# One of 32 V loads of a decode attention kernel sent as sixteen transfers of eight partitions

## The chip, the cores and the metric

The kernel runs on one core of one Trainium2 chip. The metric is the device time of one execution in microseconds. Before the change the median of three runs is 197.03 us (196.81 to 197.30). A profile of one execution on the chip belongs to it; that execution took 196.93 us.

The engines are named as in the profile: PE (matrix multiply, with PEld for its weight loads), DVE (vector), ACT (activations), POOL and SP. SP computes nothing here, its instructions issue the large DMA transfers. Sixteen DMA engines move the data. A time written as a position, such as 105.84, counts from the start of the profiled span.

## What is computed

One decode step for eight sequences. Attention over the last 1024 positions of a K/V cache with 8 heads of K and V, 16 heads of Q and a head size of 256, mixed by a sigmoid gate with a small MLP:

```python
W = min(4096, max(256, Sk // 4))                 # 1024
k = jnp.repeat(k_cache[:, :, Sk - W:, :], rep, axis=1)
v = jnp.repeat(v_cache[:, :, Sk - W:, :], rep, axis=1)
scores = jnp.einsum("bhqd,bhkd->bhqk", q, k) * (Dh ** -0.5)
p = _softmax(scores, axis=-1)
o = jnp.einsum("bhqk,bhkd->bhqd", p, v)
a = o.transpose(0, 2, 1, 3).reshape(B, Sq, Hq * Dh) @ wo
...
h = _gelu(_layernorm(x) @ w1 + b1)
b = h @ w2 + b2
g = _sigmoid((x * gate_w).sum(-1, keepdims=True))
return g * a + (1 - g) * b
```

All tensors are bfloat16. The parts of K and V that are read are 64 MB; the weights are another 13.6 MB.

## The kernel before

The work on the cache is cut into 32 units for K and 32 for V. A unit is one K/V head (`g`, 0 to 7) of two sequences (`u`, 0 to 3, `TB` = 2), numbered `n = 4 g + u`. One load brings one unit: a tile `kv` of 128 partitions, each with 16 positions of 256 numbers, 8 KB. Partition `2 r + t` holds positions `16 r` to `16 r + 15` of sequence `t`, so the source is walked as 64 blocks `r` by 2 sequences `t`, each a contiguous run of 8 KB. The tiles come from a pool of twelve (`NKV`). Only the last V unit is sent in two transfers of half the width.

All of these loads are issued by SP, in the order of the list `units` (L170 to L179): K of unit `n`, after every fourth K the part of `wo` for one head (`W`, 448 KB), then V of unit `n - 5`. V of unit 16 thus stands between K of unit 21 and K of unit 22. `issue_to` issues as many as there are free tiles: twelve at the start, and one more for each unit of K or V that the PE has used up. SP works its list in order; an instruction that waits holds all later ones.

An issue on SP waits for two things. The framework gives the transfers eight completion semaphores in turn, so a transfer waits until the one eight places before it has landed. And a load that takes a tile over waits until PE has read the tile's last content.

The main loop (L528) goes over half units, one sequence each: `transposes` turns K with the PE into PSUM, and DVE copies it out (L392, L397); `scores` multiplies it with Q (L418); once per head come maximum, exponent and sum; eleven half units later `pv` multiplies V with the probabilities (L490); once per head `o_proj` adds the head's part of the output (L515). At the end one DVE operation adds the MLP's part (L555) and two transfers store the result (L559).

ACT's queue carries four small transfers at the start (`x_sb` and `gw_sb` of eight rows, `b1_sb` and `b2_sb` of one row) and one of the two output halves at the end.

Of the kernel before, what the change touches and what calls it, by code (L numbers as in the profile page):

```python
# [16 lines left out]
def kernel(  # L17
# [15 lines left out]
    nc = tc.nc  # L33
    P = nc.NUM_PARTITIONS

    B, Sq, D = A_x.shape
    _, Hkv, Sk, Dh = A_k_cache.shape
# [4 lines left out]
    kv0 = Sk - W  # L42
# [3 lines left out]
    TB = 2  # L46
    NC = W * TB // P
# [14 lines left out]
    NU = NBU * Hkv  # L62
    NSTEP = NU * TB
    SPG = NBU * TB
    LAG = 3
    NKV = 12
    NEG = -1.0e30


# [18 lines left out]
    big = ctx.enter_context(tc.tile_pool(name="big", bufs=1))  # L88
    kvpool = ctx.enter_context(tc.tile_pool(name="kvpool", bufs=NKV))
    ktpool = ctx.enter_context(tc.tile_pool(name="ktpool", bufs=3))  # L90
# [45 lines left out]
    KV = {}  # L136

    def load(kind, n):
        t = kvpool.tile([P, NC, Dh], BF16, tag="kv", name="kv")
        src = A_k_cache if kind == "K" else A_v_cache  # L140
        g, u = divmod(n, NBU)
        parts = TB if (kind, n) == ("V", NU - 1) else 1
        w = NC // parts
        for q in range(parts):
            nc.sync.dma_start(
                t[:, q * w : (q + 1) * w, :].rearrange("p c d -> p (c d)"),
                src[u * TB : (u + 1) * TB, g, kv0:Sk, :].rearrange(
                    "t (r c) d -> r t c d", c=NC
                )[:, :, q * w : (q + 1) * w, :].rearrange("r t c d -> r t (c d)"),
            )  # L150
        KV[kind, n] = t

    nc.scalar.dma_start(x_sb[:], xf)
    nc.scalar.dma_start(
# [27 lines left out]
    def issue_to(k):  # L182
        while pos[0] < len(units):
            kind, n = units[pos[0]]
            if kind == "W":
                r0 = n * NKH * P
                nc.sync.dma_start(
                    wo_sb[n][:].rearrange("p (i j) n -> p i (j n)", i=rep),
                    A_wo[r0 : r0 + NKH * P, :].rearrange(
                        "(i p j) n -> p i (j n)", i=rep, j=NJ  # L190
                    ),
                )
            else:
                if pos[1] == k:
                    return
                load(kind, n)
                pos[1] += 1
            pos[0] += 1

    issue_to(NKV)  # L200

# [5 lines left out]
    nc.gpsimd.affine_select(  # L207
        out=cross[:], in_=cross[:], compare_op=ALU.is_equal, fill=NEG, base=0,
        pattern=[[-1, TB], [0, rep]], channel_multiplier=1,
# [145 lines left out]
    for c in range(DC + 1):  # L355
        for k in range(NQ):
            if c < DC:
                w, xs = wq_sb[:, c, k * P : (k + 1) * P], xT[:, c, :]
            else:
                h, kk = divmod(k, NQ // 2)  # L360
                w, xs = wq_t[:, kk * P : (kk + 1) * P], xT[:, DC + h, :]
# [147 lines left out]
    def o_proj(g):  # L509
        ot = OT[g]  # L510
        for i in range(rep):
            for h in range(NJ):
                k = i * NJ + h
                for j in range(CT):
                    nc.tensor.matmul(  # L515
                        A_ps[CP * j : CP * j + NB, :],
                        lhsT=ot[:].rearrange("p j (b i) -> p j i b", i=rep)[:, h, i, :],
                        rhs=wo_sb[g][:, k, j * DN : (j + 1) * DN],
                        start=(g == 0 and k == 0),
                        stop=(g == Hkv - 1 and k == NKH - 1),  # L520
                        tile_position=(0, CP * j),
                        skip_group_check=True,
                    )
# [4 lines left out]
    for n in range(LAST):  # L528
# [5 lines left out]
        g, r = divmod(n, SPG)  # L534
# [8 lines left out]
        if m >= 0:  # L543
# [6 lines left out]
            if m % SPG == 0 and m > 0:  # L550
                o_proj(m // SPG - 1)
        issue_to(NKV + done)
    o_proj(Hkv - 1)
# [36 lines left out]
```

## Time and profile before

| What | Value |
|---|---|
| median of three runs | 197.03 us |
| the profiled execution, its own time | 196.93 us |
| its span, first to last instruction | 195.1 us |
| PE busy | 166.0 us (85%) |
| DVE busy | 109.6 us (56%) |
| read from HBM | 77.68 MB, 398 GB/s over the span |
| packets of all DMA queues | 12770 |
| a K load, from issue to landing (median of 32) | 19.7 us |
| a V load (median of 31) | 18.2 us |
| the V load of unit 16 | issued at 105.84 us |

The page of the profile begins with busy times by engine, then shows the span in 40 equal slices with a digit per slice (9 stands for 90% or more), then the DMA queues with packets, bytes and share of the engines' time, then the chain of work that ended last, followed backwards from the last instruction. Views of the trace add the order of the instructions on one engine (timeline), who waited for whom (waits), and sums over chosen stretches (windows). A row of a timeline gives start, duration, engine, line, operation and tiles; SPq is SP's sequencer as it issues a transfer, and the duration is that of the issue, not of the data.

### The profile page before, as it was taken

Reading aid. Unit: us, or ns where it says so; the run is one execution under the profiler, and the core shown is the slowest. Engines: PE = TensorE matmul, PEld = TensorE weight load, DVE = VectorE, ACT = ScalarE, POOL = GpSimd, SP = SyncE. Lnnn points to the kernel's source line nnn. Section 1 sums busy time; section 2 is a strip of 40 time slices with the busy share of each in tenths; the row PEclk is TensorE's granted clock in tenths of the full one; section 3 lists DMA queues with packets and bytes.
Section 4 is the critical chain, followed back from the end, with each engine's and each line's share of the span. In section 5 each row is a group of like instructions: output and inputs, shape, how many; then the busy total and the mean of one; then the engine's idle time right before and its main releaser. Section 6 shows DMA issues by size and latency. Waiting matters only on the chain.

```text
span 195.1 us, 7576 instructions
## 1 busy us (share of the span) xinstructions
PE 166.0 (85%) x3528; PEld 155.2 (80%) x3528; DVE 109.6 (56%) x246; ACT 6.4 (3%) x13; POOL 2.7 (1%) x15
## 2 busy tenths in 40 slices
PE   0777899988799999799998997999689969898663
PEld 0665899988798899689997997889588969797561
DVE  3422189995476357745596468547384637665301
ACT  4100000000000000000000000000000000000000
POOL 5000000000000000000000000000000000000000
PEclk9999999997855559755597599559797888879555
DMA  5999999999999999999999999999999999999940
GB/s 207 410 436 422 418 417 431 422 425 417 422 425 422 422 425 423 422 420 425 427 423 418 425 423 423 422 417 426 425 422 427 420 423 423 428 423 420 404 189 8
DMA packets 12770, 78.16 MB, mean 401 GB/s; under 512 B 1330, under 2 KB 3523, under 8 KB 4164
## 3 DMA queue, kind: packets, MB, share of 16 engines
q1 hardware_dynamic: 12688, 77.67, 95.5%
q8 instruction: 27, 0.44, 0.8%
q10 hardware_dynamic: 52, 0.02, 0.1%
q14 instruction: 3, 0.02, 0.0%
HBM read 77.68 MB, written 0.01 MB: 398 GB/s over the span
## 4 chain that ended last, share of the span: by engine, by line
DMA 74%; PE 22%; SPq 1%; DVE 1%; issue 1%; ACT 0%; ACTq 0%
DMA kv<-in_A_k_cache_dram 58%; PE ktp L392 13%; DMA wo_sb<-in_A_wo_dram 9%; DMA wq_sb<-in_A_wq_dram 7%; PE grp L418 3%; PE grp L490 3%; PE A_ps L515 1%; DVE kt L397 0%; SPq L167 0%; PE grp L407 0%; DVE rz L477 0%; DVE res L555 0%; SPq L164 0%; PE grp L460 0%; SPq L159 0%
## 5 line engine op out<-in xcount | busy, mean ns | idle before, releaser
L397 DVE COPY kt<-ktp 128x1024 bf16<-128x1024 bf16 x128 | 84.8, 688 | 48.9 <-PE ktp L392 48.4
L392 PE MATMUL ktp<-ident,kv 128*128 128x128 bf16 x1024 | 89.4, 258 | 8.7 <-DMA kv<-in_A_k_cache_dram 8.7
L392 PEld LDWEIGHTS <-kv 128*128 128x128 bf16 x1024 | 77.7, 118 | 12.3 <-DMA kv<-in_A_k_cache_dram 9.4
L490 PE MATMUL grp<-e,kv 128*128 128x4 bf16 x1024 | 35.1, 165 | 5.9 <-DVE rz L477 4.6
L490 PEld LDWEIGHTS <-kv 128*128 128x128 bf16 x1024 | 32.1, 100 | 7.4 <-issue 5.0
L418 PE MATMUL grp<-qT,kt 128*128 128x4 bf16 x1024 | 36.9, 166 | 0.9 <-issue 0.5
L418 PEld LDWEIGHTS <-kt 128*128 128x128 bf16 x1024 | 34.8, 101 | 2.3 <-issue 1.0
L467 ACT ACTIVATE e<-grp 128x256 bf16<-128x256 f32 x8 | 3.1, 384 | 165.1 <-PE grp L460 165.1
L515 PE MATMUL A_ps<-wo_sb,ot 128*8 128x224 bf16 x64 | 7.0, 366 | 0.3 <-DMA wo_sb<-in_A_wo_dram 0.3
L477 DVE RECIPROCAL rz<-grp 128x16 f32<-128x16 f32 x8 | 2.0, 254 | 7.9 <-PE grp L472 5.9
L472 PEld LDWEIGHTS <-onesb 128*128 128x128 bf16 x128 | 4.7, 102 | 1.9 <-issue 1.2
L299 PE MATMUL h_ps<-yT,w_sb 128*128 128x8 bf16 x42 | 4.2, 194 | 0.8 <-DMA w_sb<-in_B_w_dram 0.8
L331 PE MATMUL b_ps<-w_sb,hT 128*8 128x224 bf16 x28 | 2.8, 388 | 2.4 <-DVE b_ps L327 2.4
L472 PE MATMUL grp<-e,onesb 128*128 128x16 bf16 x128 | 4.7, 174 | 0.0
L501 DVE TENSOR_TENSOR ot<-grp,rz 128x32 bf16<-128x32 f32 x8 | 1.5, 192 | 5.2 <-PE grp L490 5.2
L299 PEld LDWEIGHTS <-w_sb 128*128 128x128 bf16 x42 | 3.6, 152 | 0.9 <-DMA w_sb<-in_B_w_dram 0.9
L263 PE MATMUL tp<-ident,y_sb 8*128 8x8 bf16 x3 | 0.2, 170 | 4.7 <-DVE y_sb L244 4.7
L331 PEld LDWEIGHTS <-hT 128*8 128x8 bf16 x28 | 1.8, 121 | 3.0 <-DVE hT L322 2.2
L460 PE MATMUL grp<-diag,onesb 128*128 128x256 bf16 x8 | 2.6, 321 | 1.9 <-DVE diag L454 1.8
L431 DVE TENSOR_REDUCE pm<-grp 128x16 f32<-128x256 f32 x8 | 3.3, 416 | 1.3 <-PE grp L418 1.3
L263 PEld LDWEIGHTS <-y_sb 8*128 8x128 bf16 x3 | 0.2, 103 | 4.7 <-DVE y_sb L244 4.7
L515 PEld LDWEIGHTS <-ot 128*8 128x8 bf16 x64 | 2.8, 103 | 1.2 <-DVE ot L501 0.4
(77 smaller groups left out, 52.4 us busy)
## 6 DMA issues: line engine op xcount, KB each, us to landing
kv<-in_A_k_cache_dram SPq DMA_DIRECT2D x32, 1024.0 KB, 19.7
kv<-in_A_v_cache_dram SPq DMA_DIRECT2D x31, 1024.0 KB, 18.2
wo_sb<-in_A_wo_dram SPq DMA_DIRECT2D x8, 448.0 KB, 18.3
wq_sb<-in_A_wq_dram SPq DMA_DIRECT2D x3, 1024.0 KB, 11.4
w_sb<-in_B_w_dram SPq DMA_DIRECT2D x1, 1568.0 KB, 9.2
w_sb<-in_B_w_dram SPq DMA_DIRECT2D x1, 1344.0 KB, 5.9
kv<-in_A_v_cache_dram SPq DMA_DIRECT2D x2, 512.0 KB, 19.8
wq_t<-in_A_wq_dram SPq DMA_DIRECT2D x1, 512.0 KB
```

The lines of the kernel that those rows point to most:

```text
L299: nc.tensor.matmul(o, lhsT=cols(w1_sb[:, c, h * FH : (h + 1) * FH]), rhs=yT[:, c, :], start=(c == 0), stop=False,)
L331: nc.tensor.matmul(b_ps[CP * j : CP * j + NB, 0:DN], lhsT=M["hT"][:, k * NB : (k + 1) * NB] if k < NF else onesb[0:1, 0:NB], rhs=w2_sb[:, ...
L392: nc.tensor.transpose(ktp[:, c * P : (c + 1) * P], K[:, h * HC + c, j * P : (j + 1) * P], ident[:],)
L397: nc.vector.tensor_copy(kt[:, j, :], ktp[:])
L418: nc.tensor.matmul(G[g][:, s : s + RU], lhsT=kt[:, j, c * P : (c + 1) * P], rhs=qT[:, j, g, bu * TB : (bu + 1) * TB, :].rearrange("p t i - ...
L431: nc.vector.reduce_max(pm[:], G[g][:, S0 : S0 + NC * R].rearrange("p (c r) -> p r c", r=R), axis=AXIS.X,)
L460: nc.tensor.matmul(G[g][:, S0 : S0 + NC * R].rearrange("p (c r) -> p c r", c=NC), lhsT=onesb[:], rhs=diag[g % 2][:].unsqueeze(1).to_broadc ...
L467: nc.scalar.activation(e[:], G[g][:, S0 : S0 + NC * R], ACT.Exp)
L472: nc.tensor.matmul(G[g][:, Z0 : Z0 + R], lhsT=onesb[:], rhs=E[g][:, c * R : (c + 1) * R], start=False, stop=(c == NC - 1), skip_group_chec ...
L477: nc.vector.reciprocal(rz[:], G[g][:, Z0 : Z0 + R])
L490: nc.tensor.matmul(G[g][:, o : o + RU], lhsT=V[:, cc, :].rearrange("p (q j) -> p j q", j=NJ)[:, j, :], rhs=E[g][:, cc * R + bu * RU : cc * ...
L515: nc.tensor.matmul(A_ps[CP * j : CP * j + NB, :], lhsT=ot[:].rearrange("p j (b i) -> p j i b", i=rep)[:, h, i, :], rhs=wo_sb[g][:, k, j * ...
```

## The change

In `load`, one unit of V, number 16 of 32, is sent as sixteen transfers. Piece `i` fills partitions `8 i` to `8 i + 7` over their whole width of 8 KB, which is 64 KB, and reads four blocks `r` of the two sequences. The bytes and their places are the same. The other loads keep their shape; their source is only written in another way.

```diff
     NKV = 12
+
+    BY_ROWS = {("V", NU // 2)}
+    ROWS = 8
...
         g, u = divmod(n, NBU)
+        rows = src[u * TB : (u + 1) * TB, g, kv0:Sk, :].rearrange(
+            "t (r c) d -> r t (c d)", c=NC
+        )
+        KV[kind, n] = t
+        if (kind, n) in BY_ROWS:
+            for p0 in range(0, P, ROWS):
+                nc.sync.dma_start(
+                    t[p0 : p0 + ROWS, :, :].rearrange("p c d -> p (c d)"),
+                    rows[p0 // TB : (p0 + ROWS) // TB],
+                )
+            return
         parts = TB if (kind, n) == ("V", NU - 1) else 1
         w = NC // parts
         for q in range(parts):
             nc.sync.dma_start(
                 t[:, q * w : (q + 1) * w, :].rearrange("p c d -> p (c d)"),
-                src[u * TB : (u + 1) * TB, g, kv0:Sk, :].rearrange(
-                    "t (r c) d -> r t c d", c=NC
-                )[:, :, q * w : (q + 1) * w, :].rearrange("r t c d -> r t (c d)"),
+                rows[:, :, q * w * Dh : (q + 1) * w * Dh],
             )
-        KV[kind, n] = t
```

In the built program SP has sixteen instructions in place of one at that point. Each writes 8 partitions by 4096 numbers and reads 4 by 2 by 4096. Each takes the next of the eight semaphores, so piece `i` waits for the transfer eight places before it, pieces 8 to 15 wait for pieces 0 to 7, and K of unit 22 waits for piece 8. The first piece alone waits for the tile's last use by PE. On PE, the first weight load that reads this tile waits for eight semaphores in place of one. The other engines' instructions are unchanged.

## The prediction

> **What bounds the kernel now.** I read the page's head, slices and chain first, to learn which engine sets the end.
>
> ```profile
> span 195.1 us, 7576 instructions
> ...
> DMA  5999999999999999999999999999999999999940
> ...
> q1 hardware_dynamic: 12688, 77.67, 95.5%
> ...
> DMA 74%; PE 22%; SPq 1%; DVE 1%; issue 1%; ACT 0%; ACTq 0%
> ```
>
> The 16 DMA engines are full from the second slice to the 38th, and 77.67 MB on SP's queue q1 take 95.5% of their time. What makes one of these engines busy longer moves the end, unless that engine has slack. So I read the queue's pace and what its issues wait for (timeline of SP: start, duration; then SP's waits: total us, times, longest).
>
> ```profile
> 77.38 0.53 SPq L145 DMA_DIRECT2D kv<-in_A_k_cache_dram  x1
> 79.81 0.54 SPq L145 DMA_DIRECT2D kv<-in_A_v_cache_dram  x1
> 82.25 0.53 SPq L145 DMA_DIRECT2D kv<-in_A_k_cache_dram  x1
> 84.68 0.54 SPq L145 DMA_DIRECT2D kv<-in_A_v_cache_dram  x1
> 87.12 0.54 SPq L145 DMA_DIRECT2D kv<-in_A_k_cache_dram  x1
> ```
>
> ```profile
> SPq L145 <- DMA kv<-in_A_k_cache_dram: 58.4, 30, 3.5
> SPq L145 <- DMA kv<-in_A_v_cache_dram: 39.7, 21, 3.4
> ...
> SPq L145 <- PE ktp L392: 5.1, 14, 0.6
> ```
>
> SP waits for earlier DMAs (98.1 us), hardly for PE's release of a slot (5.1 us). In the built program every transfer on SP waits for the one eight places before it, so eight are in flight. Four loads are issued in 87.12 - 77.38 = 9.74 us: 2.435 us each. A load is 128 rows of 8 KB, eight for each of 16 engines, so **a row holds an engine 0.304 us**.
>
> The windows of the tail (stretch, its length, ACT's busy time, PE clock, DMA share, GB/s) show that the engines do not finish together:
>
> ```profile
> 184.00:185.00 1.00, 0.00 (x0) 0.50 0.94 382
> 186.00:187.00 1.00, 0.00 (x0) 0.50 0.55 225
> 188.00:189.00 1.00, 0.00 (x0) 0.50 0.54 209
> 190.00:191.00 1.00, 0.00 (x0) 0.50 0.14 47
> ```
>
> Half of them are through at about 185, the other half between 189 and 191; 0.14 of 16 is the last two. The final load counts as landed when the last of them is done.
>
> **The change, part by part.** (1) Removed: one issue of 0.53 us on SP, and one load's eight rows on each engine, 2.43 us of stream. (2) Added: sixteen issues of eight rows. What the trace has of eight rows is ACT's gw_sb, and the outputs at the end:
>
> ```profile
> 1.43 0.28 ACTq L154 DMA_DIRECT2D gw_sb<-in_gate_w_dram  x1
> ```
>
> ```profile
> q10 hardware_dynamic: 16, 0.00, 0.7%
> ```
>
> The first (ACT's timeline) prices an issue at 0.28 us; a piece has the three-step source of a K load (0.53), so 0.28 to 0.54. The second (DMA view of 192.5 to 195.1 us) is ACT's queue at the end, which carries one output half: 16 packets, eight rows of 448 B and eight completions. A transfer of eight rows thus used at most eight engines, while 128 rows use sixteen. How many does a piece use? In the built program its source is walked as 4 steps of 2 batch rows, its destination as 8 partitions. Eight if the destination decides, four if the source's four steps do; I take **four**, since a division that has to fit both sides can be no finer than four. The trace has no transfer whose two sides differ below sixteen.
>
> [...] No run here shows a transfer with unequal sides yet.
>
> (3) I take the four to be the same for every piece: ACT's two one-row transfers, b1 and b2, went through one engine, as the trace's packets (rows of one engine come 0.304 us apart) can be followed. They get 128 / 4 = 32 rows instead of eight. **Lower bound**, each row at 0.304: 32 x 0.304 = 9.73 us, less the 2.43 removed: +7.30. **Upper bound**: the eight rows of a piece go into eight neighbouring partitions, while in a 128-row load each engine has eight of the 128 to itself. If two engines that write into the same few partitions take turns, a row costs 2 x 0.304 = 0.608: 32 x 0.608 - 2.43 = +17.03. No 8 KB row of the trace has two engines there. I take **the middle**, 0.456 a row: 32 x 0.456 - 2.43 = +12.16. Reason: the engines reach the pieces displaced. The sixteen completions of the K load ahead of them (issued at 102.98) spread from 117.96 to 121.33 us, 3.4 us or eleven rows; the engine in front writes other partitions than the one behind for the first pieces, and meets it once pieces come only as older ones land.
>
> [...]
>
> (4) Slack: rows on an engine that would have finished early cost less. Following q1's packets engine by engine through the trace, the engine that carries b1 and b2 ends at 189.5, the last at 190.9: **-1.4** if that one is among the four. Bounds: 0 (the four hold the last one), -6 (all four end at 185).
>
> (5) SP and the eight in flight. Piece s0 is issued at 105.84, when the load eight before it has landed, and s7 only once K load 21 has landed (121.4); s8 to s15 wait for s0 to s7, and the next K load for s8. Behind SP's waits stand all later loads, and PE waits for these. With four engines it costs nothing extra: seven pieces of two rows are 14 x 0.304 = 4.3 us of queued work, longer than one issue and start (0.54 + about 0.5, as the output's 192.67 issue and its first packet show), and a piece takes 0.61 us, longer than its issue. The cover is the pieces' own slowness; without it (rival 2) SP's issues set the pace. The other twelve engines run dry and refill before the four are done. (6) PE: one weight load waits for eight semaphores instead of one; PE idles while K load 22 is late and then works at the stream's pace as before. The tail behind the last landing (191.2 to 195.1) stays.
>
> **Sum**: +12.16 - 1.4 = +10.8. Span 195.1 + 10.8 = 205.9. The profiled execution took 196.93, 1.83 outside its span, 0.10 under the median of 197.03. **207.7 us.**
>
> **Rivals.** *1, four engines without turns:* rows keep 0.304. +7.30 - 1.4 = +5.9, **202.8**. For it: every 8 KB row of the trace takes the same time whatever the other fifteen do. Against: these fifteen were in other partitions. *2, eight engines, rows at 0.304:* 16 x 0.304 - 2.43 = +2.43, no slack (the last two would be among eight more likely); or SP's nine issues s7 to s15 after 121.4: K load 22 starts moving at 121.4 + 9 x 0.28 (or 0.54) + 0.54 + 0.5 = 125.0 to 127.3, where it would have started at 121.3 + 2.4 = 123.7: +1.3 to +3.6. The larger of each pair: +2.4 to +3.6, **199.3 to 200.5**. For it: the output half used eight. Against: there both sides have eight steps. (Eight engines whose rows cost double come to rival 1's sum, 16 x 0.608 - 2.43 = +7.3.) *3, fewer than four engines, or all in turn:* two engines carry 64 rows, 64 x 0.304 - 2.43 - 1.4 = +15.6, **212.5**, and more with turns. Only the two batch rows of the source speak for it. *4, not slower:* pieces go to all engines in rotation (eight rows each, as before), and SP issues them fast enough that the queue does not run dry: 9c + 0.54 + 0.5 must stay under 2.4, so an issue c under 0.15 us. Then **197.0**. Against: the cheapest issue in the trace is 0.27 (b1, b2), and nothing shows a rotation. That the change does nothing is excluded: the built program has sixteen transfers there.
>
> **How the numbers follow.** Forecast 0.50 (205 to 212.5), rival 1 0.29 (202 to 204.5), rival 2 0.11, rival 3 0.06, rival 4 0.04. The range 200.5 to 212.5 holds the first two and rival 2's upper end, and leaves out some 0.18. About 0.3%, 0.6 us, can be told from no change. Faster 0.01, same 0.03, slower 0.96: only rival 4 does not end slower, and a quarter of it goes to a gain from a luckier slack of the engines.
>
> **What will show it.** Completions: a 128-row load has 16; the page's 12770 packets become 12818 with four engines for each piece (64 - 16 more), 12882 with eight, 13010 with sixteen. The windows after 122 us: a DMA share near 0.25 or less, and 107 GB/s without turns (4 x 8192 B / 0.304 us), 54 with full turns. SP's timeline: s7 at about 121.4, K load 22 at 121.4 plus half the stall. The tail: the last stretch no longer ends with two engines but with up to four. The prediction is wrong if the share stays above 0.9 between 120 and 135 us, or if K load 22 waits for PE instead of s8.

## The result and the profile after

| What | Before | After |
|---|---|---|
| median of six runs of each, in one comparison | 196.94 us (196.81 to 197.30) | 205.37 us (204.53 to 206.62) |
| ratio of the medians, 95% interval | | 1.0427 (1.0403 to 1.0452) |
| span of the profiled execution | 195.1 us | 203.4 us |
| K load 21, the last before the edit, landed at | 121.33 us | 122.44 us |
| K load 22, the next after it, issued at | 107.84 us | 128.59 us |
| K load 22, landed at | 127.62 us | 136.25 us |
| last load of `wo`, landed at | 191.21 us | 199.34 us |

The kernel became slower by 8.4 us. The page's head, slices, DMA table and chain, as they were shown of before:

```profile
span 203.4 us, 7595 instructions
...
DMA  6999999999999999999999961599999999999970
...
DMA packets 12818, 78.16 MB, mean 384 GB/s; under 512 B 1378, under 2 KB 3571, under 8 KB 4212
...
q1 hardware_dynamic: 12736, 77.67, 92.3%
...
DMA 51%; PE 35%; DVE 7%; SPq 3%; issue 2%; ACT 0%; ACTq 0%; DVEq 0%
```

The same 77.67 MB go over q1, but slices 24 to 26 (5 us each) are no longer full: 6, 1 and 5 tenths. The stream has one hole, and the rest of it runs as before. The packets are 48 more, which is 64 completions for the sixteen pieces in place of 16: four engines for each piece.

SP's timeline around the hole, and SP's last nine issues of pieces by tile (count, shortest, median and longest in ns, first and last start):

```profile
102.99 0.54 SPq L159 DMA_DIRECT2D kv<-in_A_k_cache_dram  x1
105.89 22.59 SPq L151 DMA_DIRECT2D kv<-in_A_v_cache_dram  x16
128.59 0.58 SPq L159 DMA_DIRECT2D kv<-in_A_k_cache_dram  x1
```

```profile
L151 SPq DMA_DIRECT2D kv<-in_A_v_cache_dram x9: 630/630/631, 122.5 to 127.8; - x9
```

Between K load 21 at 102.99 and K load 22 at 128.59 SP sends nothing but 1 MB of V. The first seven pieces are issued at the stream's pace, each when an earlier load has landed. The other nine are issued back to back from 122.45, 0.63 us each and 0.675 us apart, and K load 22 directly behind the last.

The windows (stretch, its length, ACT's busy time, PE clock, DMA share, GB/s) show what the engines do meanwhile:

```profile
118.00:120.00 2.00, 0.00 (x0) 1.00 0.76 295
120.00:122.00 2.00, 0.00 (x0) 0.78 0.49 152
122.00:124.00 2.00, 0.00 (x0) 0.50 0.17 61
124.00:126.00 2.00, 0.39 (x1) 0.50 0.15 61
126.00:128.00 2.00, 0.00 (x0) 0.50 0.28 78
128.00:130.00 2.00, 0.00 (x0) 0.50 0.23 86
130.00:132.00 2.00, 0.00 (x0) 0.50 0.96 274
```

From 122 to 130 us between two and five of sixteen engines work (0.15 to 0.28). They move 61 to 86 GB/s, less than the 97 GB/s at which SP issues (65,536 B in 0.675 us): the pieces pile up on their four engines. PE has no work at the end of it. Its waits (total us, times, longest), first the line of before, then those of after, and a row of PE's timeline after (in brackets the idle time ahead of it, and what ended that):

```profile
PE ktp L392 <- DMA kv<-in_A_k_cache_dram: 8.7, 8, 1.9
```

```profile
PE grp L501 <- DMA kv<-in_A_k_cache_dram: 5.9, 1, 5.9
...
PE ktp L403 <- DMA kv<-in_A_k_cache_dram: 5.2, 7, 1.4
```

```profile
134.43 0.56 PE L501 MATMUL grp<-e,kv 128*128 128x4 bf16 x16 [5.88 <-DMA kv<-in_A_k_cache_dram]
```

The view puts the long wait down to a K load, but L501 is `pv`, which reads V, and it goes on at 134.43, when K load 22 has not landed (136.25) and the last piece of V unit 16 has (134.08). So PE waits 5.9 us for the pieces; its wait for K load 22 is 0.46 us, ahead of a row at 136.29.

The end of the stream, the same kind of windows:

```profile
197.00:198.00 1.00, 0.00 (x0) 0.50 0.45 170
198.00:199.00 1.00, 0.00 (x0) 0.50 0.08 29
```

The last stretch belongs to about one engine (0.08 of 16). The sixteen completions of two loads, read from the trace's semaphore events in order of time, show the same engines' lag from the hole to the end:

```
K load 22, before:  122.86 to 124.80 (eight), 125.87 to 126.19 (seven), 127.62
K load 22, after:   134.09 to 134.49 (twelve), 135.02 135.06 135.24 136.25
last wo, before:    185.17 to 187.00 (eight), 189.59 to 191.21 (eight)
last wo, after:     196.24 to 198.01 (thirteen), 198.44 198.50 199.34
```

So two things add up at the end: thirteen engines are through 6.8 us later than the last engine before (198.01 against 191.21), and the slowest one is another 1.3 us behind them. The experiments take the two apart.

### The profile page after: what moved, and what is told of

The parts are those of the page before. It is cut to its first block, busy times and chain, and to the rows that moved or that the text cites. A ratio compares the mean times of both kernels' runs of the same rounds, so it can differ in the third digit from the quotient of the medians.

```text
span 203.4 us, 7595 instructions
## 1 busy us (share of the span) xinstructions
PE 172.2 (85%) x3528; PEld 161.2 (79%) x3528; DVE 110.3 (54%) x246; ACT 6.4 (3%) x13; POOL 2.7 (1%) x15
## 2 busy tenths in 40 slices
DMA packets 12818, 78.16 MB, mean 384 GB/s; under 512 B 1378, under 2 KB 3571, under 8 KB 4212
## 3 DMA queue, kind: packets, MB, share of 16 engines
q1 hardware_dynamic: 12736, 77.67, 92.3%
## 4 chain that ended last, share of the span: by engine, by line
DMA 51%; PE 35%; DVE 7%; SPq 3%; issue 2%; ACT 0%; ACTq 0%; DVEq 0%
DMA kv<-in_A_k_cache_dram 45%; PE ktp L403 20%; PE grp L501 6%; PE grp L429 6%; DVE kt L408 3%; DMA kv<-in_A_v_cache_dram 3%; DMA w_sb<-in_B_w_dram 3%; SPq L151 2%; PE A_ps L526 2%; DVE diag L465 1%; PE grp L471 1%; DVE rz L488 1%; DVE pm L442 0%; ACT e L478 0%; DVE mx L459 0%
## 5 line engine op out<-in xcount | busy, mean ns | idle before, releaser
L403 PE MATMUL ktp<-ident,kv 128*128 128x128 bf16 x1024 | 95.5, 268 | 7.1 <-DMA kv<-in_A_k_cache_dram 5.2
L403 PEld LDWEIGHTS <-kv 128*128 128x128 bf16 x1024 | 83.0, 123 | 10.9 <-DMA kv<-in_A_k_cache_dram 6.4
L501 PE MATMUL grp<-e,kv 128*128 128x4 bf16 x1024 | 35.4, 166 | 9.9 <-DMA kv<-in_A_k_cache_dram 5.9
L501 PEld LDWEIGHTS <-kv 128*128 128x128 bf16 x1024 | 32.6, 101 | 11.2 <-issue 10.8
L429 PEld LDWEIGHTS <-kt 128*128 128x128 bf16 x1024 | 35.5, 102 | 1.8 <-issue 0.7
```

Source lines behind the costliest of these rows:

```text
L403: nc.tensor.transpose(ktp[:, c * P : (c + 1) * P], K[:, h * HC + c, j * P : (j + 1) * P], ident[:],)
L429: nc.tensor.matmul(G[g][:, s : s + RU], lhsT=kt[:, j, c * P : (c + 1) * P], rhs=qT[:, j, g, bu * TB : (bu + 1) * TB, :].rearrange("p t i - ...
L501: nc.tensor.matmul(G[g][:, o : o + RU], lhsT=V[:, cc, :].rearrange("p (q j) -> p j q", j=NJ)[:, j, :], rhs=E[g][:, cc * R + bu * RU : cc * ...
```

## Experiments

Three mechanisms were in question when the expectations were written. One is the rows: engines that write at the same time into the same few neighbouring partitions take turns, and a row costs up to 0.608 us in place of 0.304. The second is SP: eight transfers in flight hold 512 KB in place of 8 MB when they are pieces, the queue runs dry, and K load 22 must wait for SP to issue nine pieces one by one. The third is the share: four engines have 32 rows to move while twelve have none. The expectations give these theories letters. Each edit is against the changed kernel, in the branch for V unit 16 where nothing else is said; each time stands beside the runs of the kernel before in the same comparison (196.80 to 196.89 us).

**e1_ports: the same pieces, written four partitions apart.**

```diff
+                i = p0 // ROWS
+                d0 = (i // 4) * 32 + i % 4
                 nc.sync.dma_start(
-                    t[p0 : p0 + ROWS, :, :].rearrange("p c d -> p (c d)"),
+                    t[d0 : d0 + 29 : 4, :, :].rearrange("p c d -> p (c d)"),
```

> The sixteen pieces read the same bytes in the same order on the same queue, but each fills eight partitions that lie four apart (partitions b, b+4, ... b+28 of a block of 32) in place of eight neighbours, so that the rows of one piece no longer share a group of four partitions. The V rows of unit 16 so stand in other partitions, and that part of the output is not the reference's. Theory A (rows of two engines take turns on the same few partitions, part of the forecast): the mean time of a row in the stretch 122 to 132 us falls from about 0.4-0.5 us to 0.31, and the time falls by 2 to 3 us from 205.4 to 202.5-203.5. Theory B (what costs is the nine issues on SP after K load 21 has landed, while twelve engines run dry): SP's rows stay 0.63 us, K load 22 is still issued at about 128.6, and the time stays within 1 us of 205.4. Theory C (32 rows on four engines, each at 0.304, nothing else): 199-201.

Measured 204.92 us, +8.1 (ratio 1.0403, 1.0385 to 1.0422), against +8.4 for the change. K load 22 is issued at 128.66. One window from the middle of the hole:

```profile
126.00:128.00 2.00, 0.00 (x0) 0.50 0.20 74
```

The hole is the same, and the rate in it too (78 GB/s there in the change): SP's nine issues held K load 22 as before, as the second theory expected. The rows themselves did change. Of the 8 KB rows that begin between 123.5 and 130 us, 50 of 61 take under 0.33 us here, against 36 of 58 in the change. Most of the others begin on three engines at once and take 0.69 to 0.90 us, more than the 0.608 of two engines that take turns; what holds them is not known. The last piece lands 1.0 us earlier than in the change (133.05), the last `wo` 0.6 earlier (198.77). So fewer turns in the hole gain little here, and not the 2 to 3 us that the first theory expected.

**e2_wide: sixteen transfers over all 128 partitions, 512 B of each row.** Every transfer spans all 128 partitions, as the loads before do, which land with sixteen completions; only SP's part of the change is left.

```diff
-            for p0 in range(0, P, ROWS):
+            wd = NC * Dh // 16
+            for q in range(16):
                 nc.sync.dma_start(
-                    t[p0 : p0 + ROWS, :, :].rearrange("p c d -> p (c d)"),
-                    rows[p0 // TB : (p0 + ROWS) // TB],
+                    t[:].rearrange("p c d -> p (c d)")[:, q * wd : (q + 1) * wd],
+                    rows[:, :, q * wd : (q + 1) * wd],
                 )
```

> Sixteen transfers again, but each over all 128 partitions and a sixteenth of the width (512 B rows), so every engine gets the same bytes as in the kernel before. Theory B (SP's nine issues after K load 21): nine issues of 0.54-0.68 us = 4.9-6.1 us plus 2-3 us until the first bytes; twelve and more engines dry in that time; 201-203 us. Theory C (rows on four engines) and theory A (turns): nothing left of either but short rows, 16 x 8 rows of about 0.025 us = 3.2 us in place of 2.43: 197.5-198.

Measured 203.73 us, +6.9 (1.0349, 1.0329 to 1.0369). SP's issues by tile and windows:

```profile
L152 SPq DMA_DIRECT2D kv<-in_A_v_cache_dram x9: 535/604/1178, 121.5 to 127.2; - x9
```

```profile
122.00:124.00 2.00, 0.38 (x1) 0.97 0.15 43
126.00:128.00 2.00, 0.00 (x0) 0.50 0.41 92
```

The same nine issues come after K load 21 has landed (121.50), and K load 22 is issued at 127.91. The hole is there although each transfer spans all partitions: **SP's pace alone costs 6.9 us**, somewhat more than expected and about the delay that the thirteen engines show in the changed kernel (6.8). Short rows can add little: a row of 512 B takes 0.027 us (median), 128 of them 3.5 us an engine, 1 us more than a load has before, and in the windows from 122 to 130 us the engines are busy for 0.15 to 0.64 of the time. That 6.9 and 6.8 are so close should not be pressed: in this trace, too, one engine ends late: the last `wo` lands on fifteen engines by 197.55 and on one at 198.55, although all large transfers of this kernel span the 128 partitions.

**e7_wide8: the same with eight transfers of 1 KB.**

```diff
-            wd = NC * Dh // 16
-            for q in range(16):
+            wd = NC * Dh // 8
+            for q in range(8):
```

(Against e2_wide.)

> Eight transfers over all 128 partitions, an eighth of the width each (1 KB rows), against sixteen in e2_wide. Theory B (the issues that SP still has to make once K load 21 has landed): one such issue in place of nine, K load 22 is issued before 123.5 us in place of 127.9, and most of the 6.9 us of e2_wide goes: 197-199. If the loss of e2_wide came from short rows or from the number of transfers as such, about half of it stays: 200-201.

Measured 198.77 us, +1.9 (1.0104, 1.0087 to 1.0120). One issue instead of nine stands between the landing of K load 21 and K load 22, which is issued at 121.99. The window in which the stream thins out most:

```profile
122.00:124.00 2.00, 0.38 (x1) 1.00 0.74 176
```

Eight issues less bring K load 22 forward by 5.9 us (127.91 to 121.99) and the time by 5.0. This is the second mechanism by its size.

**e3_rows16 and e4_rows32: eight pieces of sixteen partitions, and four of thirty-two.**

```diff
-    ROWS = 8
+    ROWS = 16
```

> Eight transfers of sixteen partitions. Each should use eight engines (the packets would be 12770 + 64 - 16 = 12818), 16 rows each. Theory B: only the last piece is issued after K load 21 has landed, so K load 22 is issued some 0.7 us later; with 2-3 us to the first bytes, +0.5 to +2: 197.5-199. Theory C: +2.43 on eight engines, nothing if these are the eight that run ahead: 197-199.4. Theory A: rows of two engines share a group of partitions, up to double: eight engines take up to 9.7 us: +2 to +5, 199-202.

Measured 203.41 us, +6.6 (1.0319, 1.0275 to 1.0363).

```diff
-    ROWS = 8
+    ROWS = 32
```

> Four transfers of 32 partitions, each over sixteen engines (packets 12770 + 3 x 16 = 12818), two rows per engine and piece, eight in all as before. Theory B and theory C: no loss, 196.9-197.3, since all four are issued before K load 21 lands. Theory A: the 32 partitions of a piece are eight groups of four for sixteen engines, so rows take up to double and the load up to 4.9 us in place of 2.43: up to +2.4, 198-199.4.

Measured 201.46 us, +4.7 (1.0237, 1.0218 to 1.0256). Windows of e3_rows16, then of e4_rows32:

```profile
126.00:128.00 2.00, 0.38 (x1) 0.50 1.02 250
```

```profile
120.00:122.00 2.00, 0.00 (x0) 0.50 1.09 225
...
126.00:128.00 2.00, 0.38 (x1) 0.50 0.94 225
```

With thirty-two rows nothing is dry, and the stream still loses 4.7 us: from about 118 to 128 us all engines are busy (0.94 to 1.09 in the windows) at little more than half the rate. The rows themselves take nearly twice as long (0.58 us on average between 119 and 127 us, against 0.31 before). This fits the first mechanism, and it costs more than the one load's own rows, because neighbours slow down as well: all 226 rows of 8 KB that begin in this stretch take 0.45 us or more, where the load has 128, and K load 21's last engine lands at 123.83 and at 121.33 before. In e3_rows16 SP is free 4.1 us earlier than in the change (K load 22 issued at 124.44, against 128.59). This trace is of the fastest of its four executions (201.84 us, the others 203.21 to 203.90), and is 3.3 us faster than the traced one of the change (205.14). By the medians the gain is 1.8. Once the queue is full again, busy engines (1.02) move 250 GB/s: there slow rows have taken back a part of what SP gave. Both times lie above all that the expectations had (up to 202 and 199.4), since these priced slow rows for the one load alone.

**e5_halves and e6_evenodd: two transfers of 64 partitions, neighbours in one, every second partition in the other.** Same number of transfers, same bytes, all sixteen engines busy (a share of 0.93 to 1.08 in the windows of both from 118 to 132 us).

```diff
-    ROWS = 8
+    ROWS = 64
```

> Two transfers of 64 neighbouring partitions, each over sixteen engines, four rows per engine and piece. Theory A (a group of neighbouring partitions takes rows at one engine's pace, so sixteen engines on 64 partitions run at half): as with four transfers of 32, a DMA share near 1.0 at about 225 GB/s for some 5 to 8 us; +2.4 to +4.7: 199.2-201.5. Theory B (SP's issues): one more issue, all given out long before they are due: 196.8-197.2.

```diff
-            for p0 in range(0, P, ROWS):
+            for q in range(TB):
                 nc.sync.dma_start(
-                    t[p0 : p0 + ROWS, :, :].rearrange("p c d -> p (c d)"),
-                    rows[p0 // TB : (p0 + ROWS) // TB],
+                    t[q : P - TB + q + 1 : TB, :, :].rearrange("p c d -> p (c d)"),
+                    rows[:, q, :],
                 )
```

> Two transfers of 64 partitions as well, but the even ones (one sequence) and the odd ones (the other), so that each transfer reaches over all 128 partitions. Same engines, same bytes, same number of issues as with two halves. Theory A: each transfer can be taken at the full pace, no stretch at 225 GB/s; 196.8-198. If instead smaller transfers as such are slow, the same time as with two halves.

Measured: halves 201.39 us, +4.5 (1.0236, 1.0220 to 1.0251); every second 196.88 us, ratio 1.0004 (0.9994 to 1.0013, ten runs): nothing lost. Windows of e5_halves, then of e6_evenodd:

```profile
120.00:122.00 2.00, 0.00 (x0) 0.50 1.08 233
122.00:124.00 2.00, 0.00 (x0) 0.50 0.97 225
```

```profile
120.00:122.00 2.00, 0.00 (x0) 0.72 1.02 430
122.00:124.00 2.00, 0.00 (x0) 0.50 1.03 422
```

This pair differs in which partitions are written together, and with that in what is read: half of the blocks of both sequences, or all blocks of one. Sixteen engines into 64 neighbouring partitions: 225 to 233 GB/s. Into 64 partitions spread over all 128: 422 to 430. **Turns on neighbouring partitions** are the likely reason. The order of the reads is not ruled out by this pair; e1_ports, which has the reads of the change and other partitions, speaks for the partitions (50 of 61 rows undisturbed there, against 36 of 58). How many partitions share a turn is not shown: the groups of four that the expectations of e1_ports and e4_rows32 count by are an assumption of their author, and 64 neighbouring partitions are sixteen such groups, one for each engine, yet the rate is halved here. e6_evenodd is a way to cut a load that costs nothing.

**e8_spread: SP's pace taken out.** Two pieces go behind each of eight earlier loads, into a part of `wq_sb` that is no longer used, so that the queue never holds pieces alone. The list `PIECES` takes the sixteen transfers in `load`, in place of issuing them.

```diff
...
-        t = kvpool.tile([P, NC, Dh], BF16, tag="kv", name="kv")
+        if (kind, n) in BY_ROWS:
+            t = wq_sb[:, 0, :].rearrange("p (c d) -> p c d", c=NC)
+        else:
+            t = kvpool.tile([P, NC, Dh], BF16, tag="kv", name="kv")
...
-                load(kind, n)
-                pos[1] += 1
+                if (kind, n) not in BY_ROWS:
+                    load(kind, n)
+                    pos[1] += 1
+                if (kind, n) == ("V", NU // 2 - 4):
+                    load("V", NU // 2)
+                for _ in range(2):
+                    if PIECES:
+                        nc.sync.dma_start(*PIECES.pop(0))
...
```

> The same sixteen pieces of eight partitions, but two after each of the eight loads ahead of V unit 16's place (V unit 12 to K unit 21), into memory that is free by then (a part of wq_sb), so that SP never has several pieces in a row and large loads are in flight beside them. Theory B (SP's nine issues in a row): the dry stretch goes and the time falls by 5 us or more, to 197-200.5. Theory C (32 rows on four engines): these engines still get 24 rows more, +7.3 less the 3.3 us and more that they run ahead: 199-201, the tail shows a share of a quarter. Theory A (turns) adds up to 3 us to it.

Measured 210.91 us, +14.0 (1.0716, 1.0689 to 1.0744): much worse than the change, and than any theory expected (up to some 204). Windows:

```profile
105.00:110.00 5.00, 0.00 (x0) 0.50 0.97 316
...
120.00:125.00 5.00, 0.00 (x0) 0.50 0.80 210
```

SP's pace alone can't be the story: a theory of SP only would have this kernel near the one before. Where pieces run beside full loads the rate falls to 316 GB/s with all engines busy, and the four that carry pieces fall behind: a K load issued at 122.31 lands on twelve engines by 129.12 and on four between 134.46 and 136.95. The share of 0.80 says that other engines run short of work meanwhile; a transfer that these four hold up keeps its place in flight, which would explain it.

**e9_split8: K load 22, V load 17 and K load 23 put between the eighth piece and the ninth.** SP's list then reaches the next large loads after one issue instead of nine. `PIECES` is as in e8_spread, the place of the tile as in the change.

```diff
...
+                if (kind, n) in BY_ROWS or (kind, n) == ("K", NU // 2 + 7):
+                    for _ in range(8):
+                        nc.sync.dma_start(*PIECES.pop(0))
```

> The sixteen pieces as in the change, but K unit 22, V unit 17 and K unit 23 are issued between the eighth and the ninth of them, so that large loads are queued before SP gives out the last eight. Theory B (twelve engines run dry while SP gives out nine pieces): the stretch at a share of 0.2 goes, K load 22 is issued at about 124 in place of 128.6, and the time falls to 199-202. Theory A in the form that the spread pieces showed (pieces beside running loads slow these by taking turns on their partitions; sixteen cost 14 us): eight of them beside the stream cost about 7, so 203-206, with a share of 0.9 and more at 210-330 GB/s while they run.

Measured 206.80 us, +10.0 (1.0485, 1.0443 to 1.0528), above both expected ranges. Windows:

```profile
124.00:126.00 2.00, 0.38 (x1) 0.50 0.82 274
...
132.00:134.00 2.00, 0.00 (x0) 0.50 0.31 111
...
136.00:138.00 2.00, 0.00 (x0) 0.50 1.13 242
```

K load 22 is issued at 122.81 and the first hole is short: between 124 and 126 us, where the change has 0.15, the share is 0.82. But the second eight pieces fill all eight places in flight again, a second hole opens at 132, and from 136 pieces run beside full loads at little more than half the rate (242 GB/s, against 422 between 126 and 128 us); V unit 16 is late, and PE waits 14.7 us for it. So this order is no way out: wherever eight pieces in a row stood in these two kernels, a hole followed.

**e10_k8: sixteen pieces on eight engines each.** A piece has eight rows of one sequence, two partitions apart, so both of its sides have eight steps.

```diff
-            for p0 in range(0, P, ROWS):
+            for q in range(TB):
+                for r0 in range(0, P // TB, ROWS):
+                    p0 = r0 * TB + q
...
-                    t[p0 : p0 + ROWS, :, :].rearrange("p c d -> p (c d)"),
-                    rows[p0 // TB : (p0 + ROWS) // TB],
...
+                        t[p0 : p0 + TB * ROWS - TB + 1 : TB, :, :].rearrange(
+                            "p c d -> p (c d)"
+                        ),
+                        rows[r0 : r0 + ROWS, q, :],
...
```

> Sixteen transfers of eight rows as in the change and at the same place, but each of one sequence alone (eight partitions two apart), so that source and destination both have eight steps. Packets 12770 + 128 - 16 = 12882 if eight engines carry each. Theory B: SP's issues as in the change, K load 22 issued at 128 to 129; the share in the dry stretch stays low; 203-205.5. Theory C (32 rows on four engines are what the end waits for): with sixteen rows on eight engines 2 to 4 us less, 201-203.

Measured 204.90 us, +8.1 (1.0408, 1.0390 to 1.0426).

```profile
DMA packets 12883, 78.16 MB, mean 384 GB/s; under 512 B 1443, under 2 KB 3636, under 8 KB 4277
```

```profile
128.00:130.00 2.00, 0.00 (x0) 0.50 0.35 98
```

The packets are, but for one, the 12882 that the prediction gave for eight engines. The pieces no longer pile up: 98 GB/s is SP's pace (65,536 B in 0.67 us), and K load 22 lands at 134.22 on its last engine, 2.0 us earlier than in the change. The time gains only 0.5 us: SP's hole stays (K load 22 issued at 128.91), and in this trace one engine falls 1.2 us behind the others between K load 22 and V load 17 and stays so: the last `wo` lands on fifteen engines by 197.70 and on one at 199.03. The queue q8, which loads instructions, moves one packet of 16 KB from 134.77 to 135.70 us; its time fits this lag, but the trace does not name its engine. Without that engine the end would come 6.5 us later than before (197.70 - 191.21), near the loss of e2_wide. So this run points to SP's pace, as the second theory expected, and not to the share of the four engines.

No version beat the kernel before; e6_evenodd equals it.

## Why the prediction was right, and where not

The forecast was 207.7 us, +10.8; measured is 205.37, +8.4, within the range and slower as forecast.

**Steps 1 and 2, four engines for a piece: right.** 12818 packets as predicted, and e10_k8 gave the count for eight engines (12883, predicted 12882) when both sides had eight steps. The choice of four, that a division has to fit both sides, was the author's inference; the two counts agree with it. The price of an issue was bounded at 0.28 to 0.54 us; it was 0.63.

**Step 3, the middle price of a row, 0.456 us: right for the rows in the hole, not for all 32, and its +12.16 partly right by luck.** The slowest of the four engines can be followed through the trace's packets in the hole, since each row starts within some 15 ns of the end of the last packet of its engine. Start and duration of its rows, in us:

```
126.082 0.499   126.577 0.351
126.929 0.599   127.517 0.379
127.896 0.600   128.485 0.379
128.864 0.598   129.452 0.358
129.811 0.479   130.286 0.341
```

Five pieces, s9 to s13, from 126.08 to 130.63 (the start of the next), 0.455 us a row, without a gap. The first row of a piece costs nearly the upper 0.608 and the second little more than 0.304. Another engine begins a row of 0.600 us at 126.89, where this one begins its 0.599, and their next rows take 0.309 and 0.379: two engines that begin a row together are both slowed to near 0.608, and less or not at all on the next, which fits turns. But other pieces had another price. The first seven begin at 117.80 at the earliest and have ended by 123.48 on three of the engines, this one among them, which is at most 0.41 us a row; and then this engine stood idle for want of issues, at least 0.4 us ahead of s7 and 0.8 us ahead of s8. The added +12.16 can be checked at the end. All four carry pieces early: the first piece has landed on them between 118.75 and 119.77, when only the eight engines that run ahead are through with K load 21 (by 119.07; the others from 120.98). Of these eight none ended later than 187.00 before; the slowest now ends at 199.34, if it is one of the four, as its unbroken lag since K load 22 says: at least +12.3. At least 1.2 us of this is the idle time, a wait for SP that the sum had at nothing, and the rows make up some 10 to 11: two errors of one to two microseconds that cancel.

**Step 4, slack of 1.4 us: mis-sized, and the term that made the sum too large.** It was taken from one engine that ends at 189.5. By the first piece's landings (step 3) all four belong to the half that ends by 187.00, 4.2 us or more before the last at 191.21. That is +12.3 - 4.2 = +8.1, the 199.34 - 191.21 of the trace; the two numbers share the 187.00, so they prove no sum, but they show which of the two terms was off. The prediction's bounds for this one (0 to 6) held it; its choice did not. One engine's end was taken for the four, although the profile before showed two halves; the engine followed there, which ends at 189.5, belongs to the other half.

**Step 5, that SP's order and the eight in flight cost nothing extra: wrong.** The text had K load 22 wait for piece s8. It waited for SP: s8 had landed by 127.14, the issue came at 128.59, right behind the last piece. The rate that was to show the rows (54 to 107 GB/s, 61 to 86 measured) could not tell them from the issues, which alone allow 97. The cover named, that pieces are slower than issues, is true only of the slowest engine and late (0.91 us a piece against 0.675 of SP); it says nothing of the twelve engines without pieces, which are fed by SP alone. For them it is rival 2's second half that holds, and that was priced too low. It had K load 22 start at 127.3 at the latest; its rows begin at 130.2 in the trace. The 2.9 us between are K load 21 landing 1.1 later than before (122.44; fifteen engines have it by 121.71, with rows of up to 0.81 us beside the first pieces, and why the last has it 0.7 later is not shown), nine issues at 0.675 in place of 0.54 (1.2), and 1.6 from the issue to the first row in a dry queue where 0.54 + 0.5 was taken (0.6). And 130.2 - 123.7 = 6.5 us is near what e2_wide shows alone (+6.9) and what the thirteen engines show in the change (+6.8).

So the change has two limits that run side by side and give nearly the same time, SP's pace (+6.8) and the rows on four engines (+8.1). They don't add up, and taking one away leaves most of the loss: e10_k8 without the pile of pieces still loses 8.1, and e8_spread with SP's pace gone 14.0, with its pieces beside full loads. The forecast named the later of the two and missed that the other stood right behind it. The gap of 2.4 us between forecast and result is not this miss but the slack of step 4 (2.8); the waits for SP stand inside the +12.3 of step 3, and there luck helped.

**Step 6 and the tail: right, but for what PE waits for.** PE waits once for 5.9 us, for the last pieces of V unit 16 and not for K load 22, and at most 1.4 us at a time for K loads; after the last landing 4.1 us remain (203.4 - 199.34), 3.9 before. Three engines end late, not four.

The rivals: 1, no turns (202.8), failed by the rows of 0.6 us in the hole. 3, fewer engines, failed by the packets. 4, not slower, failed.

What stays open: what stalls three engines at once in e1_ports, why e4_rows32 and e5_halves lose 4.6 us where one load at half pace would lose 2.4 (the neighbouring loads slow down too, but by which engines is not shown), and how the 1.3 us of the slowest engine divide between turns, its four-fold share and what sets single engines back by a microsecond in e2_wide and e10_k8.

## What to carry to other kernels

In a stream that is fed by a few transfers in flight, count what those places hold: here eight large ones kept the rate at 414 GB/s and more between 120 and 130 us, sixteen of 64 KB let it fall to 61 GB/s, and the next large load then waited for the issuer, one issue of 0.63 us at a time. If a load must be cut, cut it so that each part still reaches across all 128 partitions (every second partition here, ratio 1.0004, where two halves took 1.0236) and into few parts (eight 1.0104, sixteen 1.0349). And price each limit for the engines that it holds: here the slow rows on four engines hid nothing for the engines that only SP feeds, which ended 6.8 us late.

## What the runs showed of the hardware that was not expected

Sixteen engines that write into 64 neighbouring partitions move 225 to 233 GB/s (e5_halves, 120 to 124 us), into every second of 128 partitions 422 to 430 (e6_evenodd). An SP issue takes 0.63 us for a transfer on four engines and 0.62 on eight with eight rows, 0.68 on eight with sixteen rows, and 0.53 for a full load: fewer rows did not make SP's issue cheaper. From an issue to the first row in a dry queue it took 1.5 to 1.6 us (122.45 to 123.90, 128.59 to 130.18), and to the first landing of a small transfer 2.2 to 2.5 (e2_wide and the change). And pieces beside full loads cost more than pieces alone (+14.0 us against +8.4): 316 GB/s with all engines busy in e8_spread, and four engines up to 7.8 us behind the rest.
